# A mask product over 160 instead of 224 columns, with the scores laid out by head and a new fixed order of operations

## Chip, core and metric

The kernel runs on one core of one Trainium2 chip. The metric is the device time of one execution in microseconds (us); lower is better. The core has five engines that work side by side, each through its own queue, in order: TensorE (PE, matrix products), ScalarE (ACT, functions and copies), VectorE (DVE, elementwise work and 32x32 block transposes), GpSimd (POOL) and SyncE (SP), which mostly issues DMA transfers. They hand work to one another through semaphores.

## What is computed

Two attention branches over the same 2048 tokens of width 512, mixed by a gate `g`. The part that matters here is branch A: 64 segments of 32 tokens, one after another. Each segment puts 8 memory rows ahead of its tokens, attends over these 40 rows in 32 heads of 128, and hands its first 8 output rows on as the memory of the next.

```python
idx = jnp.arange(L)                                   # L = 8 + 32
mask = (idx[:, None] < M) | (idx[:, None] >= idx[None, :])
for s in range(n_seg):
    h = jnp.concatenate([mem, x[:, s * seg_len:(s + 1) * seg_len, :]], axis=1)
    q, k, v = (jnp.einsum('btd,dhe->bhte', h, W) for W in (Wq, Wk, Wv))
    scores = jnp.einsum('bhqe,bhke->bhqk', q, k) * scale
    scores = jnp.where(mask[None, None], scores, -1000000000.0)
    p = _softmax(scores, axis=-1)
    o = jnp.einsum('bhte,hed->btd', jnp.einsum('bhqk,bhke->bhqe', p, v), Wo)
    mem = o[:, :M, :]
    outs.append(o[:, M:, :])
...
return g * a + (1 - g) * b
```

Branch B is a causal attention in four stretches of 512 tokens with a linear memory, 32 heads of 16. It has no chain from segment to segment of 32 tokens, so its pieces can be put between those of branch A.

## The kernel before

Every piece of work is an operation with a name, an engine (or a choice of engines), a function that issues its instructions, what it reads and writes, and a cost and due time for a planner (`Prog`). The order of operations on each engine does not come from the planner's due times here: it is given outright, as a packed list in `ORDER`, which `sequences` unpacks; an operation that may run on two engines runs on the one in whose list it stands. `schedule` then walks through the lists in the planner's model of time (`LATENCY`, `TO_PE`, the costs), by which it hands out the eight PSUM banks and picks between two forms of some products. `emit` writes the instructions and the waits. So the model's constants count twice: when an order was searched for, and when banks are handed out.

**A segment** (`p_seg`), for each half `r` of 16 heads: `k`, `q` and `v` are projected (`wproj`, L1399), 4 column groups of the array side by side, copied out (`kev`, `qev`, `vev`, L999) and k and q transposed on DVE (`ktp`, `qtp`, L1464). In `p_s` one PSUM bank takes the scores:

- `H` (L1472, a helper at L1022 or L1024) multiplies a constant `neg` (-1e9 on a diagonal) with a constant `hide` (ones where a score is masked), and so writes the mask into the bank.
- `S` adds the scores: 16 products of 40 queries with the segment's own 24 tokens and 8 memory rows (L1479), and 4 products of the last 8 tokens' keys, whose projections are made four segments at a time (`rk`, `rq`, `rv`), with the last 16 queries (L1483).
- `exp` (ScalarE, L1487) turns the 224 columns into `PT`: columns 0 to 159 are the 4 heads' 40 queries against the own keys, 160 to 223 the 4 heads' 16 late queries against the remaining keys.

In `p_u`, `U` sums over the keys by a product with ones (L1502); `ln` and `rc` (ScalarE, L1506 and L1508) form the reciprocal as exp(-ln); `nrm` (DVE, L1510) and `nrr` (DVE or POOL, L1513) scale `PT`. `PV` (L1544, L1549) multiplies with the values, `OTev` copies out, `wo` (8 operations, L1298) projects back, `par` and `fold` add the partial sums, and `hm` (L1321) writes the memory rows of the next segment, on which its `k`, `q` and `v` depend.

**Branch B** runs in 16 units: projections `bk`, `bq`, `bV`, logits `bL` (L1139), exponentials `bE` (L1157), triangle masks `bM` on POOL (L1163), `bPV` (L1180), and outputs. Its `bL` pieces share PSUM banks with `PV` in many segments.

**The start.** The weights arrive in the first 50 us or so. PE meanwhile runs 64 products without use (`warm`), early work of branch B and the first projections. `tables` (L782) sets up ScalarE's function table for exp, ln and copies.

Of the kernel before, what the change touches and what calls it, by code (L numbers as in the profile page):

```python
# [8 lines left out]
ALU = mybir.AluOpType  # L9
# [6 lines left out]
    "c-nPZ2S5|&+kf6%lFK3qLs4;|f`D6aQ>!9cC$?gtPPAA@t<+t`g(4MKwQg-4t+wdjja6JI?g1+9i56E~pb!#5a_@cbU6RXP@Ix}Vd+wRPXT9wRxdE(TE7QZ&WVFaSec^ly"  # L16
    "W0(U;D`4TH*ZW(weG>Aa#pLw&KXpC!y~?{dy}d0aZNZOAUtd1a<wTo)(=rQ_mdnh_@jv;t3*XRd$FJ7cS#WkO1e@{#3#w@2nT2&9FI`mtN?1Ki0~6=Z8Ld7VeKZ=D#BSHb"
    "T#3jC+5oE?M4xN_<)rCpuT>VHSzSg?3k@0HK;%g(0svHLbIw9|c4t_1z>KgQmPVYOb}Tot?Xb2@sY?^jM6R{T!)}9bl{>Zng}P7bC}nzp^Fh9W=f1pUq^>vjE2qIya=k3Z"
    "VggW`9~w?B+Yh04PK;Uy5uJ!U;C~K5Yo9}{FAY`L5Jh>}?O?eK5ys+cZDnvKQhlULy#p;=q%go|-Jc_Ut&D=HVzsCuk9tu>DljkGjO#v!!de9u2w4{^Fg^f%vhY|dQrHaS"
    "8Zv*ZE-zNy*H;J4?K;Y<Z|b%(gUUg97|LS~1H>w93fteK+MhF%YX(c(3y6HGLvQ3<o+mI(0{CUJEt8=cq5=@Y*R?GMo1J<Djc*2?gU?Sv%@E>o$4|Ar(8eD?juZ?-bkJ2O"  # L20
    "Z04dsdx=W^^nbAp@71pjuLRQq0G7pmb6Q7PX>IYxDsO7ZA44sQDkrYf!Lk_(U`ocnse&5$08MHgjAkf`Suz*QUO-vOG-ZTR{WM?zK$c)yry0=o7;L)C5Uyz9OqCoys?El7"
    "vu=J`+5CC`+nQs6=o|;>jSis~^G9xoVGi^|UKUk}+`9-gcFInHQkG5b|FuovN|c4d9yh(M423?dSpbFL1Kxpf1;TFv3cW+TX3s!_1wZUbj9>LVz)^%~E7B?|6d%=3gYWyj"
    "tz}-@zmW+R!Hfkba|G(I^IGnx-;z*M$Yub!o%-POUaqK6eXRD%D}5#{c<lNFIALl{RH$LnzVNNM6{!EHrpwE`O1#vm0fV*yj27Hg2jIzzxIzu0d|y{BFV!<<_|G3yO1oLD"
    "-UuxrH#}?&z<7amdT?;)U(JRRoKaeUGVm_anrM&#Y#M9-ZKA+7WsYIpL|#pc%Az)F<#Uo$KLeze0w`(09tD6^so^j{(=x`QD+L0WUnVV?Rkj3va+_22P<ZYa-bAFKRCgq>"
    "iRD3cE@_?x!@ZXF>%nl&=QBZW`pR)D3k}nM<9NQS2djFITj}fbUfnbwm4a4l3cDTlFb!a~z<MIA8?~f+qb$xIZ!0Kl@?s-;-{pjQPxsDnYs;YR3!e(SFOpX){kHEA`O$I!"
    "Hx|=C5<yd@bnEIvUT<U0>KWQ*_^417RC@&>6{WzrDDsTD<)zls63C;fpa&fB+^_+2_HjsEGm~TtL8-A=C7TC3ADKWI4DeDAy)g{hjc5ZY2vLj|m?v&1@h0glE7f&6scwC)"
    "{Z<%qMbKaz#J7)`GJ>$xTC6Pq9t1rsBLz$OmZZzr)g)T4_4`H=9Y+4alg9)6^WjkWcs>n$E6hC(sp*?Fp!=!MVM8++iI+cQLn}}NDRuzIAO}+RT-(R_t4EGSh00*XctZu)"
    "snp~h!)BzUK&lYkQ6#)8yb^ZuN-HYNdRrOE8=XzQaBkw-mmA%L*C~6moAy2=V-$3$j^rU2?G=`YoAQPPoXfvor3Uy;FfRz;esIEOt;uM~=&Rj6$m_X}YBgNlSf-QP>?F_s"
    "`nF8D|J4-Yy7a0113T|Gj%n6^8wr|Msg6W#=g49LHrXaf(5y;O-Xs*w1?E?t#-4=)im}lhZre?CIVhXmkd+#OZ)-Aohdz2uC~62=KLn_+yB5uPf+E!%R2IXJ=?uw)w%6?~"
    "x!Yx+PFn7&361}$Mc$RwCrwh==vMh)DUZCox1V8i>Wzid7EVu_PC%4#d$|zsOIwDu9@AwChYb?%-(ZBAE>fE{9M~GeJ$D8X*3U9WTND-rNuhFDUaI11?r4BN2d@PYEH6M?"  # L30
    "Q**{ZmD-S=tBIHEk%DDL8Y1>R?EO)Y>pgYpn<@k-jKZs!(#bz+NXT>#0?n@)Xg<p>e*ojo2`qmCNc-!?KdA0=#;cfC$xDa_v{XjSuCFy)2Tn~{1~5xdbJ9E5y#44=J_bwX"
    "m`U~$q$ALp#5x}Ckq^BIRyadS6e_yHqy?M&@R#<U<mM59S8e#UZ*9<US;+ZaSE{0I_QydbuYw*l%?~?7DEbJre*?s2C}&s@rLd@!x#8tE8yoTf8p7RB(Aq6<4*GFnIz>n$"
    "Ir=~-Ftt=5E2?t3^(AO?vAQ?u{v>y7q?xNpsZ`!<Oqezo_@DY<fR6eD@uYYo1-V+TT0dG|thH0CVT{`T%T92orBCn7_oO)JXe-g>?@{II)uRfks~?3HubEpyZr^LN=OH9J"
    "8BbdXQ#X9GdThrWhs!8V3!1Lr(DkUX{f-@=1xI?e14lg>dUiT_5H^!`jtE#<!6i~0NcuF+hT3JiQW8)9z=AReE8uz89FjJ@?=VOGHj`3s<g($P-kdk8f~$>@#Jd~vf?_Dz"
    "riBkmzTLsg0F}%{$^mg0Pjm(%k8aOlx@GeT5P2bG-g`Bq&ME<a6Db(i_RcL3U^RFYKzrlCc#`6zbjm-1nx2qeqBiRw@Kv>Eq%puuQGy2@3<B(!40u@4#G_|BlFqr)-8hlq"
    "&qN0|z7P}jWbmkoz5EeC8$oPsfTv&Py>Jz54t1Yh=3qycH-9O#Y`$dsJ?YHBEYne7ffK4>wkCjP<>>NFVYjCWJO=`7+qd(WOSaBV7lDezMP27nebVh+R(S0=$<?1D3Jb-J"
    "3?zPr3VVyI9HD)4lE96Og&(NB!_o4|q@jQC1(3ZnT7gV9{&I`T#S5A0IK{oLs*_tNJ3r3YY07z@=8Y)i3Jg?v^QO@)XmqQkm-VBb8&q_qIx<L~gC2*Xj{CHeJ0CegUR0e!"
    "5b_e6u)H%y-;l%!yF%&)<RoBp_qnC{EExV8qjfk4ieUGT7<K9a6=!lWin@YPWb<obx#17MM*Gs(0Qj@_*zY=YEXl{wV7US9?}V-%55&(kb|jK1Q>O;YsXkz*Wq5=SY+XM="
    "!5GP<1@JT2$_)szY5Xk#uTfo2E5U9dSF{IkBAGaiYbJt44>oA@5NS=bGGlg=;nG27QmV+MM*L%7k*mR$(;dJ!c2{7tJdQ}Fgd+bkjXiyqS1CN<$3Z<IH2Z^11xQ;m_A=Av"
    "nr+d78OzFPo-la{!qK;?Fz>1&eMwa)Qr&AsG$yL_#xJZ)VGH&B;38F{Lh?8QjUTScflBA#Xrfc+k&Bmlasv;iPKEEQYO`mm5!N*!Ls-BIy_yrkJ-RW;)Sjf3j;N=E>x~Ek"  # L40
    "wSFsMDf7n&q~j_w0R$&hlkyAjbCJ;{p-QRW+qyh^&iZ-NX_>a9HOXRQNsnBf#BRCQ8W64p{{0RRvch1_b0#uZ;jiIYw?nj3SNk7}?h~@R(b&sr0Fj7QGCUM+5RmDghHzwd"
    "N)Am5OtbX+PDN5287Gv)s?NV!)0Bf;Lw7pU-u^0Rzl6KQzYbnD;M5;D6ptbk5YfI!)hUmWnG6JP$6*#XHJnx#8~K2d&5PQm`{>K_;x4Gs)Rm=;9juB}M6Z>TWLTHJ-^xr|"
    "jP%bAOys?2x8(F8A~sZo8>FclNvt@r<(noDcTZ_k>uECAzSm9SJ#3;?2y69lHHt{)6(p9)@HhA|GQVzMGk&NBo8q~r7o-Eyls4s2!r5ByK9^LQ+H3Jpg$Qw=O*+i{k-$C2"
    "L#f;#)08gQ$%Ub+GYUqcMh4^`t_#l`;nQ;$39m^Jcp7r~k_3h@%L*tQgD8E8R^xC02M1Fd5wdKz!ilMkQ(+P^I<z+tR@!DZ^e}=q&{l5D4Ttm<p!qAo>Y(8fI_`9bD^`k6"
    "1101&Ar)IQbtA6Y^|+Ha?{3|+<e&$^l#W<aq|#v-m<&i)dS~Ar9#`)|!4jEIBpOJf)#0MT(-BY^WH`T^1h_jsPU+Onpcn|M>R>M>W1!#*&cr_Wk)mAYRE%VV)(0yoC-4aG"
    "ZWl><`Z<*%DZpocy}&-1PKa@_*_=dtkcq!zT+i{0bY43k#X|9%Ie-xw1sKtCNaCa8aD&#5a{CgLns#rh62vg%zMRY!1ol%$Y>GP-BY#t+y2^S#L~~je+3)F%v`nNeyGRzv"
    "Cv{=?rsn5g_P%9Nz4aTq6`HmiyBhUMo}Ds#@%DjvP;(C?Uc0jSLMiMSZ2NoYXA8HlXn#EF+}7W&;~M`_{<dQ8T7`p1VeP)Y?o(*sJ7z(<^G#KDHQ95HfBvok?3;QYD7bhf"
    ";?4v(JfNBdtX>TE!8WB_ex-AE7pQ5ae@{?hjJ;JA)U^nI69VJTks8uGm|LOVGP&FUUN#+>mKgl|B%2N=t*ZYf3ntzSQ(bL_(<ghAp~5Do@;YVw2)cU>ZCZ>A1H2c`ppJDv"
    "Qmq40T6e(UBjYg<@E^?5ZImf+R<DD(OD<@8KdDXH>|9tnaj}i2e)#cy_l~oonqXC_8c38CnDW})AKH9OnMtVhHl+fe?3((zWca3C{r}k-8~e<HE0AVp%IvYLm!IzcoTiRJ"
    "_al8Wzk*$4kvI)+Yha`=taYzRMcO<)e0>IJj9Wd#<ua{}Hr9DcL;c5fl?ZoP-TG1snwpnV5&$#yuK2KkE>|GC7p203Hr;OdOP$O?{b0}C#i6)Dhtb#--o$B#p;z#-crx>)"  # L50
    "CLcRN*e;%EggI#yDpFI8Wj-Vi4)ny{Hf_c7pA5O-O)(LY8--7xF7nVn-^R^I`wQZORD`OacK_ns_th)Zv%B^fv_1ZB^^UJYY_bX+FuH;UA@>#dG<<i@3uX4Mu3Da?K$!8K"
    "o}!g|U2hIy7)RVd_(d2dZp#7`2S2u1Ho^DZV&W&ecV-NgxH)0>sEXaiK|r31XuFm39YuUPX!Q28SXrjUp*Ow11=tEDm!pp|RK2DUKR`bUFPc@V!Ny6;<UR<FOs4VY7l4^{"
    "HV<SJWcCFe$}Y^^`7)58hl5I^yVQs+Q`g17g?2aZH)wl?q{<)TY@v@hw5Z!!#;r(N17iRZ0)kI=InizY-2IBLAp?ru>>^o3)O^_pQxuh#Q@RA2C~>*U?)|=oRbH##s$&iB"
    "4KYFfLO4fb8Y8>+^)Q;6w0t<g4z2MyG;2B_x%hPxW;S$d$3#4$sAJik+tu7P<#8zI=;WG-oae`!7`g)1PbbFnsD|O&Y;|AFyq`rTm?}hhH3RorUmCVWA4<ueZ&?U>KO*W;"
    "AUAQy<k!O6u8bNKJNtSY=rp?<Fy!&`ovd=|_*aW3?;fY(&JyNL_pbk}V!~Pj#GRCpsYl1DNl_;O*<$wrGze+QQCY5b|8WtSoibytyd0Df*U2|mWv2)TN#<QukPdLDY8Qk5"
    "y{2TWy3-Kj{LevYtG~5#&HWwyU&9_4xnY9JV$%@qNsN<LE%+JLq6%7?L5Y7G?rqcMw#e!U2T9~J0-mQPrz$v)hBYW49_<X-`fe)t=!>wSKG<K7a0GfeJV{aVBe5ZOt7GM&"
    "so0S8D^PMTl(0F}CTnx8c^+E6C4N32`SJ0vy(5B*8%<|mI|<e7Uu=_C$YJWofZ53_!QiI?y40!H=}vnMs1F=Sq%jY@&h68v8!fKBi5<R4&U?zvRS&O%dR1f)bSm{Ik79~C"
    "(M=Dv$rJNu+Bq&%<GwjJ;xe>BG;JmV8S>2O&e^^2p+0)}aDae_Sv!FNEd}qY+f)XS8H@cnanB(1PH4rWrj#K&+6)^1ns8MXPK<u<r?egEi_fAclpPrmqiC7;c*sE@c{TPI"
    "J7rH<aIwR?(^+4{oU%p@3rgPYd!*xeXf-AOER4&$9MlExw+*PX6QgR3chQq(0RLN8gZ`i~+&cXGi;6j4wes$Ix<hXjGi7Ie@9z&i2<mk=q(C|D%Y6_rs6%@g*s(2~KXn)P"
    "?sR@h@^_bV)2`+8Non3I>+;2w_t%Y$>o`1gSwi^tw~~epyPg}bDOo=C_)PqMBS2>u@-!IF+SEw7W^9$J_37QqF2@f?JJ;0i6<NQ`JFD;cA^2A^;V=I3N{1RFPSG1`_G^08"  # L60
    "r^hjX>DO>9{j5Ptm>>OhtK2K+x2)@2^I7-IpRa5hGrH94*Z3n(w$JIF1zTHxJC5$DZ(H6t`o+}#7rM6?`a^JidiBFKBQ}hT%gFyX@2^LD)~-$3`)>K~>(G`SwCYdWhSLdj"
    "7W9S|sqnDDw$}Mf-0<~nVHrgC>3mK#46e5LY{>ETC~fc67K@-qpCw;4tbZ(ZYfi_(QO93bt$lrII<(sp5P1f=G-}i-ejNIJLva7c53(*cU)?TmPBp*y?_ltsFAfwZp6V99"
    "2w+X___3qo+Tpk=!%)r78(9jo(+|g}!f@o8anEx4G{Xx4);CF<OxLa-_uu&+)}fhAGD07pT#z#@Z{m=njnj*JE*igV!Mo=tzJOYdj0t%-9896fvGkd!It5+nDo3Ly&1~6z"
    "d53VnxA_g>-nUKQ9=+rrTGj5%(%RWp81jdO4*t!m?fX7ydCzIP`Y%O`Q$gPR`lRecb<#qaOty?)W6U5dT;ylW+&OdS0IY@~qt<U3wq>x4t>BIWHUU`2l27j3KA|`4?bD4r"
# [504 lines left out]
FLEX = ("c32", "full")  # L569
# [13 lines left out]
class Kernel:  # L583
# [194 lines left out]
    def p_init(self):  # L778
        P, C, M = self.P, self.C, self.M
        op, dma = P.op, P.dma  # L780
# [640 lines left out]
    def p_seg(self, s):  # L1421
# [13 lines left out]
        def bank():  # L1435
            return P.slot("A")
# [31 lines left out]
        def p_s(r, i, prio):  # L1468
            rb = bank()

            def f_hide(pe, m):
                return self.mm(pe, m, pb[rb.b][:, 0:224], self.neg[:, :], self.hide[:, :], True, True, skip_group_check=True)  # L1472
# [137 lines left out]
```

## Time and profile before

| | |
|---|---|
| runs | 833.68, 831.29, 832.03 us; median 832.03 |
| span of the profiled execution | 828.3 us |
| DMA, first 52 us | busy share 0.99, 373 GB/s |
| mask product, tiled form (L1022, 128x224) | x504 matmuls, mean 259 ns a row |
| function table loads on ScalarE | 2, of 1.28 us, at 1.31 and 12.86 us |
| nrr on POOL, on DVE (L1513) | x90 at 371 ns; x38 at 238 ns |

The span runs from the first to the last recorded instruction; the time of a run has something more around it. A row of the profile gives an instruction's line, engine, operation, tiles (out<-in) and its partitions by elements. A matmul's row lasts until its results are out, but the next may start much earlier, so for PE the step from start to start is what counts.

### The profile page before, as it was taken

To read this page: it belongs to the slowest core of one execution; us is meant where nothing else is said; L and a number is where in the kernel's file an instruction comes from. 1 tells how busy PE (TensorE), PEld (TensorE's weight loads), DVE (VectorE), ACT (ScalarE), POOL (GpSimd) and SP (SyncE) were. 2 spreads that over 40 slices of the span, in tenths; PEclk is the share of its full clock that TensorE was granted. 3 is DMA by queue.
4 is the path that set the end of the run, shared out by engine and by line. 5 is a ranking of instruction groups with operands and counts; after the bars stand their busy time and mean duration, and the time that the engine had idled before them with its cause. 6 is when DMAs were issued, how large, how long until landed. Compare 5 with 4: busy or idle time off the path is not lost.

```text
span 828.3 us, 53292 instructions
## 1 busy us (share of the span) xinstructions
PE 804.8 (97%) x24456; PEld 521.1 (63%) x24474; DVE 617.3 (75%) x1398; ACT 564.1 (68%) x1279; POOL 262.3 (32%) x576
## 2 busy tenths in 40 slices
PE   8999999999999999999999999999999999999987
PEld 4445666766666566666767666666666665666654
DVE  4788668769778767778687687776877767876775
ACT  4677766777767666676667766677666677767663
POOL 3552231223323323223233233423223223323340
PEclk9999999999999999999999999999999999999999
DMA  9982111111111111111012111100111110010001
GB/s 344 413 248 58 41 26 39 38 45 31 42 30 30 33 28 43 28 34 46 26 33 53 38 27 31 34 22 11 49 38 39 34 26 8 13 26 21 21 21 36
DMA packets 71701, 45.63 MB, mean 55 GB/s; under 512 B 50046, under 2 KB 69942, under 8 KB 69942
## 3 DMA queue, kind: packets, MB, share of 16 engines
q1 hardware_dynamic: 70422, 41.18, 17.2%
q8 instruction: 192, 3.15, 1.6%
q10 hardware_dynamic: 1056, 1.05, 0.4%
q14 instruction: 31, 0.25, 0.1%
HBM read 30.72 MB, written 8.87 MB: 48 GB/s over the span
## 4 chain that ended last, share of the span: by engine, by line
PE 86%; DVE 4%; ACT 4%; DMA 3%; issue 1%; SPq 1%; POOL 1%; DVEq 0%; POOLq 0%; ACTq 0%
PE pb L1399 47%; PE pb L1298 17%; PE pb L1022 7%; PE pb L1139 3%; PE pb L1544 3%; PE pb L1180 2%; PE pb L1024 2%; DMA st<-in_A_mem_dram 2%; PE pb L1502 2%; PE pb L1479 1%; DMA out_dram<-stg 1%; PE pb L1228 1%; ACT rc_sb L1508 1%; ACT rc_sb L1506 1%; PE pb L1483 1%
## 5 line engine op out<-in xcount | busy, mean ns | idle before, releaser
L999 ACT ACTIVATE st<-pb 128x512 bf16<-128x512 f32 (+2 forms) x313 | 149.1, 494 | 103.5 <-PE pb L1399 78.3
L1157 ACT ACTIVATE PTB<-pb 128x640 bf16<-128x640 f32 x240 | 158.4, 703 | 35.2 <-PE pb L1139 30.3
L1399 PE MATMUL pb<-Wv_sb,hT 128*32 128x512 bf16 x2048 | 162.7, 380 | 0.1
L1399 PE MATMUL pb<-Wq_sb,hT 128*32 128x256 bf16 (+1 forms) x3072 | 139.4, 308 | 0.1
L1399 PE MATMUL pb<-Wk_sb,hT 128*32 128x512 bf16 x2048 | 133.2, 379 | 0.2
L1298 PE MATMUL pb<-Wo_sb,OT_sb 128*32 128x256 bf16 x4096 | 131.9, 273 | 1.0 <-DVE OT_sb L999 0.4
L1513 POOL TENSOR_TENSOR PT_sb<-PT_sb,rc_sb 128x64 bf16<-128x64 bf16 x90 | 33.4, 371 | 248.2 <-ACT rc_sb L1508 239.7
L1163 POOL TENSOR_SCALAR_AFFINE_SELECT PTB<-PTB 128x512 bf16<-128x512 bf16 x120 | 77.8, 649 | 105.7 <-ACT PTB L1157 99.2
L1298 PEld LDWEIGHTS pb<-Wo_sb,OT_sb 128*32 128x32 bf16 x4096 | 100.7, 96 | 15.6 <-ACT OT_sb L999 3.8
L1399 PEld LDWEIGHTS pb<-Wq_sb,hT 128*32 128x32 bf16 x3072 | 83.3, 97 | 39.8 <-issue 1.9
L1464 DVE STREAM_TRANSPOSE QT_sb<-st 128x256 bf16<-128x256 bf16 (+1 forms) x192 | 94.4, 510 | 17.1 <-ACT st L999 15.2
L1464 DVE STREAM_TRANSPOSE KT_sb<-st 128x512 bf16<-128x512 bf16 x128 | 89.4, 700 | 12.2 <-ACT st L999 10.5
L1399 PEld LDWEIGHTS pb<-Wk_sb,hT 128*32 128x32 bf16 x2048 | 57.7, 97 | 43.0 <-issue 1.7
L999 ACT ACTIVATE OT_sb<-pb 128x320 bf16<-128x320 f32 (+1 forms) x140 | 58.2, 428 | 37.7 <-PE pb L1549 36.4
L999 DVE CAST OT_sb<-pb 128x320 bf16<-128x320 f32 (+1 forms) x120 | 56.9, 479 | 31.4 <-PE pb L1549 29.6
L1399 PEld LDWEIGHTS pb<-Wv_sb,hT 128*32 128x32 bf16 x2048 | 52.8, 97 | 17.8 <-DVE ao L1328 0.6
L1506 ACT ACTIVATE rc_sb<-pb 128x160 f32<-128x160 f32 x128 | 38.9, 304 | 35.5 <-PE pb L1502 34.5
L1321 DVE CAST hT<-pb 128x32 bf16<-128x32 f32 x63 | 12.0, 191 | 66.7 <-PE pb L1022 66.5
L1487 ACT ACTIVATE PT_sb<-pb 128x224 bf16<-128x224 f32 x128 | 45.7, 357 | 17.3 <-PE pb L1483 12.6
L999 DVE CAST V_sb<-pb 128x512 bf16<-128x512 f32 x65 | 44.5, 685 | 9.9 <-PE pb L1399 8.9
L1510 DVE TENSOR_TENSOR PT_sb<-PT_sb,rc_sb 128x160 bf16<-128x160 bf16 x128 | 42.7, 333 | 8.1 <-ACT rc_sb L1508 6.8
L999 ACT ACTIVATE stg<-pb 128x512 bf16<-128x512 f32 (+1 forms) x68 | 37.9, 559 | 13.6 <-PE pb L1399 9.6
(204 smaller groups left out, 1468.9 us busy)
## 6 DMA issues: line engine op xcount, KB each, us to landing
Wv_sb<-in_A_Wv_dram SPq DMA_DIRECT2D x4, 1024.0 KB, 11.3
Wk_sb<-in_A_Wk_dram SPq DMA_DIRECT2D x4, 1024.0 KB, 20.2
Wq_sb<-in_A_Wq_dram SPq DMA_DIRECT2D x4, 1024.0 KB, 26.1
Wo_sb<-in_A_Wo_dram SPq DMA_DIRECT2D x4, 1024.0 KB, 21.3
rest_v<-stg SPq DMA_DIRECT2D x112, 32.0 KB
rem_v<-rest_v SPq DMA_DIRECT2D x28, 128.0 KB, 3.1
a_rows<-ao SPq DMA_DIRECT2D x63, 32.0 KB
stg<-a_rows SPq DMA_DIRECT2D x15, 128.0 KB
```

The source lines that it names most:

```text
L999: self.P.op(("act", "dve"), (lambda a: a.activation(dst, src(), ACT.Copy), lambda d: d.tensor_copy(dst, src())), reads=reads, writes=write ...
L1022: ins = pe.matmul(out[32 * c:32 * c + 32], lhsT[:, 32 * c:32 * c + 32], rhs, start=start, stop=stop, tile_position=(0, 32 * c), **kw)
L1139: ins = pe.matmul(pb[slot.banks[i]][:, base + a - lo:base + b - lo], KT[r0:r1, 128 * kc:128 * kc + 128], Q[r0:r1, t0 + a:t0 + b], start=Tr ...
L1157: P.op("act", (lambda dst=dst, src=src: lambda a: a.activation(dst, src(), ACT.Exp, scale=0.25))(), reads=[pair], writes=["%s%d_%d" % (nam ...
L1163: P.op("gp", (lambda pt=pt, ii=ii: (lambda g: g.affine_select(pt, pt, ([[0, len(ii)]] if len(ii) > 1 else []) + [[1, 128]], ALU.is_ge, 0.0 ...
L1298: ins = pe.matmul(pb[so.b][p0:p0 + 32, 0:256], tok(r, g, l), self.Wo[:, h, 256 * d:256 * d + 256], start=(r == 0 and g == 0 and l < 2), st ...
L1399: ins = pe.matmul(self.pb[sl.b][32 * g:32 * g + 32, 0:hi - lo], x[:, c, 0:32], cols, start=(c == 0), stop=(c == C - 1), tile_position=(0, ...
L1464: op("dve", (lambda dst=dst, src=src: lambda d: d.transpose(dst, src))(), reads=["st%d%s" % (i, tag)], writes=["%sT%d%s" % (kind, r, tag)] ...
L1487: op("act", lambda a: a.activation(PT[:, r, :], pb[rb.b][:, 0:224], ACT.Exp, scale=SCALE), reads=[rb], writes=["PT%d" % r, "PT%dr" % r], n ...
L1506: op("act", lambda a: a.activation(rc[:, r, :], pb[rb.b][:, 0:160], ACT.Ln), reads=[rb], writes=[rr], name="ln%d_%d" % (s, r), cost=t_act( ...
L1510: op("dve", lambda d: d.tensor_tensor(PT[:, r, 0:160], PT[:, r, 0:160], rc[:, r, :], ALU.mult), reads=[rp, rr], writes=[rp], name="nrm%d_% ...
L1513: op(("dve", "gp"), tuple((lambda e: e.tensor_tensor(rest, rest, late(rc[:, r, :]), ALU.mult)) for _ in range(2)), reads=[rp + "r", rr], w ...
```

## The change

1. **Layout.** `PT` and the scores' bank hold, for each of the 4 heads, 56 columns: first the 16 late queries against the remaining keys (`rest`), then the 40 queries against the own keys (`mine`). Every product that reads or writes them goes through these views.
2. **Mask product.** The queries that mask nothing (the memory's and the last 8 tokens' against the own keys) now lie at the end of each head's columns. `H` writes columns 0 to 39 of each 56, 160 columns in all, and `hide` shrinks to 160.
3. **The planner's model.** The hand-over times grow by 0.02 us on PE, ScalarE, DVE and POOL (`LATENCY`), and by 0.015 from ScalarE to PE; the cost of `H` falls to 0.072 and that of `nrr` on POOL rises to 0.42.
4. **The order.** `ORDER` is another list. Compared by operations: PE has the same 2914 in another sequence, tiled forms for 127 of the 128 `H` (126 before). ScalarE has 1258 operations (1283 before), DVE 1466 (1398), POOL 529 (572), SP 367 as before, in much the same sequence. `nrr` runs 58 times on POOL and 70 on DVE (90 and 38 before). `tables` stands after 66 operations in ScalarE's list (after 3 before). The built program has six function table loads on ScalarE where it had two: the first at the start, then ahead of `ln0_0`, of `bE1_6_3`, of `ln0_1`, of `rc0_1`, and `tables` itself between `OTev0_0` and `OTev0_2`.

```diff
-    LATENCY = {"pe": 0.22, "act": 0.04, "dve": 0.04, "gp": 0.1, "sp": 2.0}
-    TO_PE = {"pe": 0.0, "act": 0.015, "dve": 0.06, "gp": 0.05, "sp": 0.0}
+    LATENCY = {"pe": 0.24, "act": 0.06, "dve": 0.06, "gp": 0.12, "sp": 2.0}
+    TO_PE = {"pe": 0.0, "act": 0.03, "dve": 0.06, "gp": 0.05, "sp": 0.0}
...
-        self.hide = t("hide_sb", [128, 224])
+        self.hide = t("hide_sb", [128, 160])
...
-        hide = [("hide", self.hide[0:32, lo:hi].rearrange("p (h q) -> p h q", h=4)) for lo, hi in ((0, 160), (160, 224))]
+        hide = self.hide[0:32, :].rearrange("p (h q) -> p h q", h=4)
+        hide = [("hide", hide[:, :, lo:hi]) for lo, hi in ((16, 40), (0, 16))]
...
+        def by_head(t):
+            return t.rearrange("p (l q) -> p l q", l=4)
+
+        mine, rest = [by_head(PT[:, r, :])[:, :, 16:56] for r in range(2)], [by_head(PT[:, r, :])[:, :, 0:16] for r in range(2)]
...
-                return self.mm(pe, m, pb[rb.b][:, 0:224], self.neg[:, :], self.hide[:, :], True, True, skip_group_check=True)
+                return self.mm(pe, m, by_head(pb[rb.b][:, 0:224])[:, :, 0:40], self.neg[:, :], self.hide[:, :].rearrange("p (h q) -> p h q", h=4), True, True, skip_group_check=True)
...
-                        ins = pe.matmul(pb[rb.b][32 * g:32 * g + 32, l * L:(l + 1) * L], KT[:, 16 * r + 4 * g + l, :], QT[:, 16 * r + 4 * g + l, :],
+                        ins = pe.matmul(pb[rb.b][32 * g:32 * g + 32, 56 * l + 16:56 * l + 56], KT[:, 16 * r + 4 * g + l, :], QT[:, 16 * r + 4 * g + l, :],
...
-                    ins = pe.matmul(pb[rb.b][32 * g:32 * g + 32, 160:224], Kr[:, h0:h0 + 4].rearrange("p h k -> p (h k)"), QT[:, h0:h0 + 4, 24:40],
+                    ins = pe.matmul(by_head(pb[rb.b][32 * g:32 * g + 32, 0:224])[:, :, 0:16], Kr[:, h0:h0 + 4].rearrange("p h k -> p (h k)"), QT[:, h0:h0 + 4, 24:40],
...
-                    for k, (dst, src) in enumerate(((o[:, 0:160], PT[:, r, 0:160]), (late(o[:, 0:160]), PT[:, r, 160:224]))):
+                    for k, (dst, src) in enumerate(((by_head(o[:, 0:160]), mine[r]), (late(o[:, 0:160]), rest[r]))):
...
-            op("dve", lambda d: d.tensor_tensor(PT[:, r, 0:160], PT[:, r, 0:160], rc[:, r, :], ALU.mult), reads=[rp, rr],
+            op("dve", lambda d: d.tensor_tensor(mine[r], mine[r], by_head(rc[:, r, :]), ALU.mult), reads=[rp, rr],
...
-               writes=[rp + "r"], name="nrr%d_%d" % (s, r), cost=(0.235, 0.33), prio=prio)
+               writes=[rp + "r"], name="nrr%d_%d" % (s, r), cost=(0.235, 0.42), prio=prio)
```

`PV` reads `mine[r]` and `rest[r]` in the same way. The 67 lines of `ORDER` become 63 others.

## Prediction

> **What bounds the kernel now.** I read the page first, then the timelines of TensorE (PE) and ScalarE (ACT) over single stages, then the waits.
>
> ```profile
> span 828.3 us, 53292 instructions
> PE 804.8 (97%) x24456; PEld 521.1 (63%) x24474; DVE 617.3 (75%) x1398; ACT 564.1 (68%) x1279; POOL 262.3 (32%) x576
> PEclk9999999999999999999999999999999999999999
> PE 86%; DVE 4%; ACT 4%; DMA 3%; issue 1%; SPq 1%; POOL 1%; DVEq 0%; POOLq 0%; ACTq 0%
> ```
>
> PE is busy 97% of the span at full clock and is 86% of the chain that ended last; no other engine passes 75%. Busy hides small stalls, since a matmul's row lasts longer than the step to the next one. So I read the steps, in PE's timeline of a middle segment:
>
> ```profile
> 309.30 0.27 PE L1022 MATMUL pb<-hide_sb,neg_sb 128*32 128x224 bf16 x4
> 309.39 0.27 PE L1479 MATMUL pb<-QT_sb,KT_sb 128*32 128x40 bf16 x16
> ...
> 310.40 0.39 PE L1399 MATMUL pb<-Wv_sb,hT 128*32 128x512 bf16 x4
> 310.62 0.27 PE L1502 MATMUL pb<-PT_sb,ones_sb 128*32 128x160 bf16 x8
> 310.71 0.39 PE L1399 MATMUL pb<-Wv_sb,hT 128*32 128x512 bf16 x4
> ```
>
> A row lasts 0.27 or 0.39, but the next starts 0.09 or 0.22 later: four column groups run side by side, and columns set the step. Laid beside the operations in their planned order, the trace gives each step: 95 ns for a mask product of 224 columns, 215 for four matmuls of 512, 97 for a sum U (160 and 64 columns). Take each step at the low tenth of its kind (operation, arrangement of the array, arrangement of the next): together 779.7 us. What is over that is 43.5 us of stalls: 5.7 before 48 us, 1.0 from 48 to 65, 34.0 from 65 to 800, 2.9 after. So a column taken away counts almost in full, and so does any new stall.
>
> **The change, part by part.** I take the sum against the span, 828.3; the median shown, 832.03, lies 3.7 above it, for what lies around the span.
>
> *Mask product.* From 224 to 160 columns. The steps 95 (224 columns) and 215 (512) differ by 120 ns over 288 columns, 0.417 ns each; 64 columns are 26.7 ns, and 128 products give 3.4 us. Lower end nothing (a step that only uncovers a wait), upper end 3.4. I take -3.4, since nearly all 126 tiled products are at 95 or 96 ns, with no wait in them.
>
> *Layout.* PT is now read and written in runs of 40 and 16 with a stride of 56. On PE the late score block already reads its queries in runs of 16 (L1483, 196 ns a row) and the sums' second product reads runs of 64 (L1502, 193): no price. On VectorE (DVE) the product L1510 takes 333 ns for 160 elements and L1513 238 for 64, whose rc operand already comes in runs of 16: 1 ns an element both ways, no price. On GpSimd (POOL) L1513 takes 371; the nearest copies are 280 (96 elements) and 435 (256, strided), so -0.09 to +0.06 each. It is off the path but where PV waits for it: some 26 stalls, 3.3 us together, so -2 to +2; I take 0.
>
> *The order.* All 2914 PE operations remain, in another order. Priced with the same steps, the new list is 779.4 without the mask cut, against 779.7 (arrangement switches, about 107 ns each, go from 388 to 385): -0.3. Stalls are the open item. For each hand-over I added up the PE work between producer and consumer, in both orders, and what it lacks of the time the hand-over took in the trace (low tenth of all):
> scores to U: 2.1 us lacking in all before, 1.5 after; U to PV: 11.0, 10.1; v to PV: 6.5, 4.7; last wo to fold: 2.8, 1.6; PV to wo: 4.0, 3.6; fold to the next k or q: 0.8, 1.0; q and k to scores: 3.2, 3.3.
> Together 30.4 against 25.8, 15% less. Of the stalls, some 22 us end with a hand-over from ACT, DVE or POOL; 15% of these is -3.4. Bounds: +3 (25 copies leave ACT and 32 of the L1513 products leave POOL for DVE, which gets 68 operations, some 25 us, and would be 78% busy: transposes wait in its queue), and -8 (a third of 22).
>
> *The table loads.* This the diff does not say. The operation that sets up ScalarE's function table stood fourth in its queue and now stands after 66 others, behind the first softmax. In the built program ScalarE has six table loads where it had two: one at the start, as before, and five in segment 0: ahead of ln0_0, ahead of the exponential that follows (bE1_6_3), ahead of ln0_1, ahead of rc0_1, and the set-up itself between OTev0_0 and OTev0_2. The planner has no cost for the first four. In the trace of before, in ScalarE's timeline:
>
> ```profile
> 11.54 1.30 ACT L1157 ACTIVATE PTB<-pb 128x640 bf16<-128x640 f32 x2 [8.95 <-PE pb L1139]
> 12.86 1.28 ACT L782 ACT_TABLE_LOAD   x1
> 14.19 1.30 ACT L1157 ACTIVATE PTB<-pb 128x640 bf16<-128x640 f32 x2
> ```
>
> The load starts where the exponential ended (12.84) and takes 1.28; there it cost nothing, as the next input came at 14.13. In segment 0 ScalarE and PE run so:
>
> ```profile
> 48.96 0.40 ACT L1487 ACTIVATE PT_sb<-pb 128x224 bf16<-128x224 f32 x1
> 51.22 0.30 ACT L1506 ACTIVATE rc_sb<-pb 128x160 f32<-128x160 f32 x1 [0.33 <-PE pb L1502]
> ...
> 53.81 0.30 ACT L1506 ACTIVATE rc_sb<-pb 128x160 f32<-128x160 f32 x1
> 54.15 0.34 ACT L1508 ACTIVATE rc_sb<-rc_sb 128x160 f32<-128x160 f32 x1
> 54.49 0.44 ACT L999 ACTIVATE OT_sb<-pb 128x320 bf16<-128x320 f32 x1
> ```
> ```profile
> 48.11 0.28 PE L1479 MATMUL pb<-QT_sb,KT_sb 128*32 128x40 bf16 x16
> ...
> 58.34 0.39 PE L1298 MATMUL pb<-Wo_sb,OT_sb 128*32 128x256 bf16 x8
> ```
>
> From S0_0 (48.11) to the last wo of the segment (58.34) PE takes 10.2 us, 9.4 of it work; ScalarE has almost no gap. With the new order, from S0_0 at X: exp0_0 ends at X+0.8; two exponentials to X+2.0; load to 3.2; ln0_0 to 3.55; load to 4.8; bE1_6_3 to 5.3. Its triangle mask on POOL (0.65) and a hand-over (0.145) let bPV1_1 start at X+6.15, where PE has come to X+2.8: 3.3 us idle. U0_1 follows at X+7.0; on ScalarE rc0_0, bkexp2, two exponentials and exp0_1 last to X+7.5, load to 8.7, ln0_1 to 9.05, load to 10.3, rc0_1 to 10.7, OTev0_0 to 11.0 (wo0_0 waits, PE idle 2.3 more), load to 12.3, OTev0_2 to 12.75; wo0_4 goes at X+12.8, the last wo at X+13.8. PE's work in this stretch is 7.9 in the new order. Stall 5.9 against 0.8: +5.1. PE works in order and its work after is the same, so nothing gives it back. Queued behind each load is all of ScalarE: exponentials, evictions, and through them DVE and SP's stores. Lower end 2.6 (only the two loads between an ln and its exponential bite), upper end 6.4 (five whole loads).
>
> Sum: 828.3 - 3.4 - 0.3 - 3.4 + 5.1 = 826.3 in the span; with 3.7 around it **830.0 us**.
>
> The Trainium skill, "ScalarE: Activation LUTs", section "What ACT_TABLE_LOAD costs", gives about 1.28 us for the load, which the trace confirms, and adds a drain of 1.38, 2.66 a switch. In the row above the load begins 0.02 us after the exponential ended and the next instruction 0.05 after the load, so no such drain shows; by the page's figure five would be 13.3, and the sum about 837.
>
> **Rivals.**
> *A, the forecast:* loads bite by some 5 us, stalls shrink by some 3; 827.5 to 832.
> *B, the order gains more.* The covers shrink evenly and the big stalls go too: 23 of over 0.3 us between 65 and 800 us make 11.8 us. Gain 8 rather than 3.4: 825.4. For it: short covers fall in most kinds. Against: many of the 23 end with no engine's hand-over, and so are not the order's to remove.
> *C, the loads hide.* ScalarE reaches a load while it would wait for PE anyway. Two or three hidden: 2.6 instead of 5.1, 827.5; for it, loads need no input; against, ScalarE's queue in segment 0 is full.
> *D, slower: the table switches starve PE.* If a switch also empties the pipeline, up to one 0.70 exponential each, five give 3.5 more; and if the idle of 3.3 us lowers PE's clock, 3.4 us at half clock cost 1.7, twice 3.4: 830.0 + 6.9 = 836.9. It decides once idle in segment 0 passes some 8 us. Against: in 22 to 26 us PE was busy 2.9 of 4 us and the granted clock stayed 1.00. The Trainium skill, "TensorE: Matmul & The Clock Gate", Part 1, lets the clock fall to half after an idle window of about 3.4 us; only the tail of this trace shows it (0.84 after the last matmul).
> *E, slower: DVE's load.* Its added 25 us make the transposes late in each segment: 3 us more stalls rather than 3.4 less, 836.4.
>
> **How the numbers follow.** Chances: A 0.47, B 0.20, C 0.13, D 0.12, E 0.08. Within 0.3% (2.5 us, 829.5 to 834.5) is about what a measurement of this kernel can tell from no change. A gives same 0.30, faster 0.12, slower 0.05; B and C faster 0.30, same 0.03; D and E slower 0.17, same 0.03: faster 0.42, same 0.36, slower 0.22. Range 825.0 to 836.5, which leaves out the ends of B and D; A alone is 827.5 to 832.
>
> **What would show it.** The mask product's step falls from 95 to about 69 ns, all else of PE's steps as before. ScalarE's timeline shows six table loads, five of them in some 10 us in segment 0, and PE's busy share falls there, with idle before L1180 and L1298 that before has not. From 65 to 800 us PE's stalls are about 30 us instead of 34. I am wrong if the loads lie in time ScalarE waits anyway, if the granted clock dips below 1.00, or if L1464 starts later after its copy than now.

## The result, and the profile after

The kernel became slower. The median of four runs is 839.59 us (838.47 to 840.74); the kernel before, run beside it, took 831.92 (831.29 to 833.68). The ratio is 1.008, 95% interval 1.0054 to 1.0106: some 7 us more, where 2 us less was forecast. The profiled execution is the run of 838.47; its span is 836.7, so about 1.8 us lie outside the span. (The forecast put 3.7 there. Before's span of 828.3 thus belongs to an execution of about 830.1, 2 us quicker than its median. Single executions of one kernel spread by some 5 us, so below medians decide the size and a profile only the place.)

The page of after, the same lines as shown of before:

```profile
span 836.7 us, 53305 instructions
PE 806.3 (96%) x24492; PEld 526.1 (63%) x24492; DVE 636.5 (76%) x1466; ACT 559.0 (67%) x1258; POOL 242.6 (29%) x533
PEclk9999999999999999999999999999999999999999
PE 84%; DVE 4%; ACT 4%; issue 3%; DMA 3%; SPq 1%; POOL 1%; DVEq 0%; POOLq 0%; ACTq 0%
```

Nothing new bounds the kernel: PE still leads, VectorE is at 76%, the clock's digit is 9 in every slice. One share has grown: "issue", time in which PE waited for nothing that the profile shows, is 3% of the chain instead of 1%.

PE's rows (start, duration, engine, line, operation) in a middle segment of after show the edit itself doing what it should:

```profile
319.83 0.26 PE L1019 MATMUL pb<-hide_sb,neg_sb 128*32 128x160 bf16 x4
319.90 0.62 PE L1396 MATMUL pb<-Wq_sb,hT 128*32 128x256 bf16 x16
...
321.65 0.26 PE L1019 MATMUL pb<-hide_sb,neg_sb 128*32 128x160 bf16 x4
321.72 0.44 PE L1019 MATMUL pb<-V,phiK 128*32 128x136 bf16 x16
```

The next operation starts 0.07 us after the mask product, 0.09 before. By all rows the step is 69 ns against 95. With each step at the low tenth of its kind, as in the forecast, PE's work fell from 779.7 to 776.0 us. The stalls grew from 43.6 to 55.0: +5.4 up to the last `wo` of segment 0, +6 after it.

ScalarE in segment 0 of after:

```profile
50.68 1.28 ACT L1508 ACT_TABLE_LOAD   x1
51.97 0.30 ACT L1508 ACTIVATE rc_sb<-pb 128x160 f32<-128x160 f32 x1
52.29 1.28 ACT L1154 ACT_TABLE_LOAD   x1
53.59 0.44 ACT L1154 ACTIVATE OT_sb<-pb 128x320 bf16<-128x320 f32 x1
...
56.22 1.28 ACT L1508 ACT_TABLE_LOAD   x1
57.52 0.30 ACT L1508 ACTIVATE rc_sb<-pb 128x160 f32<-128x160 f32 x1
57.84 1.28 ACT L1510 ACT_TABLE_LOAD   x1
59.13 0.34 ACT L1510 ACTIVATE rc_sb<-rc_sb 128x160 f32<-128x160 f32 x1
59.38 0.42 ACT L996 ACTIVATE OT_sb<-pb 128x320 bf16<-128x320 f32 x1
59.81 1.28 ACT L778 ACT_TABLE_LOAD   x1
61.11 0.44 ACT L996 ACTIVATE OT_sb<-pb 128x320 bf16<-128x320 f32 x1
```

Five loads of 1.28 us, where the forecast put them. What follows each starts 0.01 to 0.02 us after its end. From `S0_0` to the last `wo` PE took 13.8 us, as the forecast had it (X+13.8), against 10.2 before.

The waits of PE after the first 65 us are the surprise. Two stretches of the weight-load rows of after and before (the last bracket is the idle time and what ended it):

```profile
301.23 0.13 PEld L1019 LDWEIGHTS pb<-xT,wkB_sb 128*32 128x32 bf16 x5
302.83 0.10 PEld L1019 LDWEIGHTS pb<-xT,wkB_sb 128*32 128x32 bf16 x3 [1.47 <-issue]
302.84 0.32 PEld L1295 LDWEIGHTS pb<-Wo_sb,OTr_sb 128*32 128x32 bf16 x8
```
```profile
316.36 0.65 PEld L1399 LDWEIGHTS pb<-Wk_sb,xr 128*32 128x32 bf16 x16
317.98 0.39 PEld L1022 LDWEIGHTS pb<-fold_sb,st 128*32 128x32 f32 x16 [0.97 <-DVE QTm L1062]
```

In the first, PE stops in the middle of one operation, after five of its eight products, whose data are all there: 1.47 us for nothing that an engine owes it. In the second an engine is named that had long been done. Both lie at the same place in another count. Count PE's instructions in order: a product is two (load of weights, matmul), one of the f32 fold four, a wait on a semaphore that is an instruction of its own one (335 on PE in the built program of after; the other waits ride on a product). Then the long stops of this kind stand at numbers that leave 193 or 194 when divided by 256, in both kernels, over the whole span. The page has the matching queue:

```profile
q8 instruction: 192, 3.15, 1.6%
```

192 packets, 3.15 MB, or 16 KB each: one for each block of 256 instructions. Laid beside the block ends of after, the packet that starts after one block end is what PE needs at the next: it had landed at least 1.2 us before PE went on, at every block end, and no packet is fetched two blocks ahead. For the stop above: block end at 298.32, packet from 300.09 to 301.45, PE on at 302.83. So a block has a floor: from its start to the packet's start (0.4 to 2.0 us in nine cases of ten), the transfer (0.9 to 1.4), and 1.2 more, about 3.4 us on average and up to 5. PE's own time for a block, without that wait, is 4.0 at the middle and 3.3 for the shortest twentieth. Where the block is quicker than its packet, PE waits.

The Trainium skill, "Runtime: NRT & Kernel Launch", section "Instruction fetch mechanics", describes blocks of 256 instructions fetched by a queue of the engine's own, and calls the cost of crossing into the next "mostly hidden". The block size agrees with the count; the cost does not: up to 1.5 us at one crossing here.

Added up after 65 us, the waits at block ends (the gap in a profile wherever the packet had landed less than 1.7 us before) are 7.1 us in before and 16.2 in after. That is a reading; the experiments test it.

### The profile page after: what moved, and what is told of

Read it like the earlier page. It is cut to its first block, busy times and chain, and to the rows that moved or that the text cites. A ratio compares the mean times of both kernels' runs of the same rounds, so it can differ in the third digit from the quotient of the medians.

```text
span 836.7 us, 53305 instructions
## 1 busy us (share of the span) xinstructions
PE 806.3 (96%) x24492; PEld 526.1 (63%) x24492; DVE 636.5 (76%) x1466; ACT 559.0 (67%) x1258; POOL 242.6 (29%) x533
## 3 DMA queue, kind: packets, MB, share of 16 engines
q8 instruction: 192, 3.15, 1.6%
## 4 chain that ended last, share of the span: by engine, by line
PE 84%; DVE 4%; ACT 4%; issue 3%; DMA 3%; SPq 1%; POOL 1%; DVEq 0%; POOLq 0%; ACTq 0%
PE pb L1396 46%; PE pb L1295 17%; PE pb L1019 7%; PE pb L1136 3%; PE pb L1545 2%; PE pb L1177 2%; DMA st<-in_A_mem_dram 2%; PE pb L1021 2%; PE pb L1504 1%; PE pb L1481 1%; PE pb L1485 1%; DVE V_sb L996 1%; PE pb L1225 1%; ACT rc_sb L1508 1%; PE pb L1550 0%
## 5 line engine op out<-in xcount | busy, mean ns | idle before, releaser
L996 ACT ACTIVATE st<-pb 128x512 bf16<-128x512 f32 (+2 forms) x302 | 143.8, 496 | 106.0 <-PE pb L1396 89.6
L1396 PE MATMUL pb<-Wv_sb,hT 128*32 128x512 bf16 x2048 | 159.0, 380 | 0.0
L1396 PE MATMUL pb<-Wq_sb,hT 128*32 128x512 bf16 (+1 forms) x3072 | 142.0, 308 | 0.5 <-DVE hT L1318 0.3
L1466 DVE STREAM_TRANSPOSE QT_sb<-st 128x256 bf16<-128x256 bf16 (+1 forms) x192 | 94.7, 510 | 12.1 <-ACT st L996 10.3
L996 DVE CAST OT_sb<-pb 128x320 bf16<-128x320 f32 (+1 forms) x116 | 54.8, 478 | 20.6 <-PE pb L1550 19.5
L1514 POOL TENSOR_TENSOR PT_sb<-PT_sb,rc_sb 128x64 bf16<-128x64 bf16 x58 | 20.6, 355 | 165.0 <-ACT rc_sb L1510 164.0
L1568 POOL COPY OTr_sb<-OT_sb 128x256 bf16<-128x256 bf16 x55 | 23.0, 419 | 94.6 <-DVE OT_sb L996 61.2
```

Source lines behind the costliest of these rows:

```text
L996: self.P.op(("act", "dve"), (lambda a: a.activation(dst, src(), ACT.Copy), lambda d: d.tensor_copy(dst, src())), reads=reads, writes=write ...
L1396: ins = pe.matmul(self.pb[sl.b][32 * g:32 * g + 32, 0:hi - lo], x[:, c, 0:32], cols, start=(c == 0), stop=(c == C - 1), tile_position=(0, ...
L1466: op("dve", (lambda dst=dst, src=src: lambda d: d.transpose(dst, src))(), reads=["st%d%s" % (i, tag)], writes=["%sT%d%s" % (kind, r, tag)] ...
L1568: op("gp", lambda g: g.tensor_copy(own[:, :, 8 * (s % 4):8 * (s % 4) + 8], OT[:, :, :, SEG:L].rearrange("p g h k -> p (g h) k")), reads=[" ...
```

## The experiments

Each was timed beside the kernel before; ratios are to it, with 95% intervals.

| kernel | median us | ratio | waits at block ends after 65 us, in its one profile |
|---|---|---|---|
| before (in the three sets) | 832.2, 832.9, 832.9 | 1 | 7.1 |
| after | 839.6 | 1.008 (1.0054 to 1.0106) | 16.2 |
| `a_tables` | 833.9 | 1.0009 (0.9992 to 1.0025) | 12.9 |
| `b_tables` | 837.7 | 1.0068 (1.0049 to 1.0088) | 10.4 |
| `b_layout` | 832.2 | 0.9998 (0.9984 to 1.0012) | 11.2 |
| `a_oldlayout_t` | 834.1 | 1.0015 (0.9999 to 1.003) | 9.9 |
| `b_layout2` | 830.3 | 0.9966 (0.9947 to 0.9986) | 8.9 |
| `b_cols40` | 826.1 | 0.9928 (0.9898 to 0.9957) | 10.3 |
| `a_t_plus64` | 845.2 | 1.0142 (1.0109 to 1.0174) | 25.8 |
| `a_t_minus12` | 828.7 | 0.9952 (0.9938 to 0.9966) | 10.1 |
| `a_t_minus24` | 827.7 | 0.9925 (0.9896 to 0.9954) | 9.4 |
| `a_t_minus36` | 826.6 | 0.9935 (0.9913 to 0.9957) | 9.5 |
| `b_l2_plus64` | 845.8 | 1.016 (1.0135 to 1.0184) | 23.9 |
| `b_l2_minus24` | 830.5 | 0.9975 (0.9959 to 0.9992) | 9.5 |

**The table loads.** One operation moved in ScalarE's list, out of after and into before:

```diff
+        q = out["act"]
+        q.insert(3, q.pop([o.name for o in q].index("tables")))
         self.ops = out
```

In `b_tables` the place is 66.

> The kernel after, with one operation (tables) put back to fourth place in ScalarE's list; everything else as in after. Theory T (the late set-up brings four more table loads, and the stall of segment 0 with them, and nothing later gives it back): two loads in ScalarE's timeline, PE's stalls up to the last wo of segment 0 fall from 11.9 us to about 6.8, median 839.6 - 5.1 = 834.5 us, still above before by about 2.5. Rival (PE would be as late without the loads, since later waits swallow the gain): 839 or so, with the 5 us turning up again as stalls after segment 0.

> The kernel before, with the same operation moved to place 66, as in after. Theory T: six loads, five of them in segment 0, median 832.0 + 5 = 837 us. Rival (the loads bite only in the new order of ScalarE's queue): 832 to 834.

Both as theory T had it: 839.6 falls to 833.9 without the late set-up, and before rises by 0.68% (5.7 us) with it. PE's stalls up to 65 us fall to 6.5 from 11.9 in the profile. The windows of after and of `a_tables` (bounds, length, then busy us of PE, PEld, DVE, ACT and POOL; clock, DMA share, GB/s) show what else came with the loads:

```profile
52.00:56.00 4.00, 2.31 (x53) 1.28 (x57) 1.39 (x4) 3.97 (x8) 0.58 (x2) 0.88 0.83 234
56.00:60.00 4.00, 3.40 (x68) 1.19 (x60) 1.21 (x4) 3.92 (x7) 0.64 (x1) 0.69 0.24 54
```
```profile
52.00:56.00 4.00, 4.00 (x131) 2.37 (x132) 3.27 (x9) 2.43 (x7) 1.09 (x3) 1.00 0.87 255
56.00:60.00 4.00, 4.00 (x128) 2.56 (x124) 2.04 (x7) 2.42 (x5) 1.51 (x3) 1.00 0.38 77
```

ScalarE is full while PE is busy for little more than half of the first window, and the granted clock falls to 0.88 and 0.69, which is 3.4 us at 0.5. In `a_tables` it stays 1.00 there. The same holds beyond these two profiles: the mean clock of an execution is 0.996 to 0.998 in the four of after and 0.994 to 0.996 in the six of `b_tables`, and 1.00 in all twelve of `a_tables`. In the profile of `b_tables` the half clock lasts 6.8 us, from 57.6 us on. From `S0_0` to the last `wo` PE takes 13.8 us in after and 8.7 in `a_tables`, 5.1 more with the loads; in the old order it takes 16.9 in `b_tables` and 10.2 in before, 6.7 more.

**The layout and the mask product alone**, in the order of before; then the order alone, in the old layout.

`b_layout` is after with `ORDER`, `LATENCY` and `TO_PE` of before. `a_oldlayout_t` is before with those three of after, and `tables` at place 3. `b_layout2` is `b_layout` with two more costs of before (the planner's cost of `H`, and that of `nrr` on POOL):

```diff
-            op("pe", f_hide, reads=["neg", "hide", "st%d" % i], writes=[rb], name="H%d_%d" % (s, r), cost=0.072, prio=prio, mode=FLEX)
+            op("pe", f_hide, reads=["neg", "hide", "st%d" % i], writes=[rb], name="H%d_%d" % (s, r), cost=0.1, prio=prio, mode=FLEX)
...
-               writes=[rp + "r"], name="nrr%d_%d" % (s, r), cost=(0.235, 0.42), prio=prio)
+               writes=[rp + "r"], name="nrr%d_%d" % (s, r), cost=(0.235, 0.33), prio=prio)
```

> The new layout and the mask product of 160 columns in the order of operations of before, with the planner's constants of before; two table loads. Theory: the product's step falls to 69 ns and 128 of them give 3.4 us, stalls as before: 832.0 - 3.4 = 828.6 us. Rival 1 (what a column saves comes back as a wait for the next hand-over or the next block of instructions): 831 to 832. Rival 2 (strided reads of PT cost VectorE or GpSimd something): above 832.

> The new order and the new constants of the planner, with the old layout and mask product of 224 columns, and the table set-up early: the order alone. Theory F (PE takes its instructions in blocks of 256, and in the new order the ends of the blocks fall where PE runs through a block too fast, some 6 us more than before between 65 us and the end): 839.6 - 5.1 + 3.4 = 838 us, with gaps of PE of 0.4 to 1.6 us at every 256th instruction. Rival H (the forecast's own term: hand-overs shrink by 3.4): 832.0 - 3.7 = 828. Rival L (the stalls come from the new layout): 832.

> Again the new layout and the mask product of 160 columns in the order of before, now with every cost in the planner as in before, so that banks and waits are those of before and only the columns and the layout differ. Theory F (a block of 256 instructions takes PE at least 3.2 to 4.8 us, by when its fetch starts and lands; time saved inside a block that is already at that floor is lost, time saved in the others is kept): of 182 blocks some 15% are at the floor, so some 0.5 of the 3.4 us is lost, and another 0.6 as a longer wait ahead of S: 832.2 - 2.3 = 829.9 us. Rival P (the plan's changed banks cost b_layout its gain): 828.8. Rival Z (a column of the mask product is worth nothing at all, because PE waits for what follows): 832.2 again.

`b_layout` gained nothing, a miss. Its planner, given a shorter `H`, had handed out other banks and put in one wait instruction more on PE (342 instead of 341). With the plan of before, `b_layout2` gains 0.34%, 2.8 us of the 3.4 (1.2 to 4.4 by the interval): rival Z is out, theory F and rival P both fit. Why the other banks and the wait cost some 2 us was not traced further. The order alone, at 834.1, is near neither 838 nor 828. Theory F's figure counted on the layout's full 3.4 us, of which 0.2 shows in this order (834.1 and 833.9); that the order alone is no gain, as rival H had it, is plain. Rival L's 832 lies within this run's interval; but in the new order the old layout is no faster than the new (834.1 and 833.9), and in the old order the new layout gains or is level, so the layout does not bring the stalls.

**The value of a column.** The same instructions in the same order, with 40 of the 224 columns. The mask of the other columns is left out, and the products of `S` that now come first there start their columns (`start=True`, in the part not shown):

```diff
-                return self.mm(pe, m, pb[rb.b][:, 0:224], self.neg[:, :], self.hide[:, :], True, True, skip_group_check=True)
+                return self.mm(pe, m, pb[rb.b][:, 0:40], self.neg[:, :], self.hide[:, 0:40], True, True, skip_group_check=True)
...
```

> The kernel before, with the old layout, whose mask product writes 40 of the 224 columns (the mask of three heads in four and of the late keys is left out; the first product into each other column starts it afresh). Same instructions in number and order. The product's step should fall from 95 ns to about 30: 128 x 65 = 8.3 us less work. Theory F: about 75% of it arrives, 832.2 - 6.2 = 826 us. Rival Z: 832. If b_layout2 shows no gain and this one does, the loss lies in the new layout and not in the columns.

The step fell to 28 ns, 8.5 us less work; 0.72% or 6.0 us of it arrived (3.6 to 8.5 by the interval). So about seven tenths of the time saved at this product reaches the end, in agreement with theory F's 75%, though the interval is wide; a column is not worth nothing.

**Where the blocks end.** A few products without use near the start are cut into more pieces or issue fewer, so that every later block end moves along the list of operations.

```diff
...
-                return pe.matmul(pb[sw.b][:, 0:512], self.phiK[:, 0, :], self.phiQ, start=True, stop=True)
+                n = 1 if isinstance(pe, Count) else {16: 16, 0: 16, 9: 3}.get(i, 1)
+                for j in range(n):
+                    lo, hi = 32 * j, 32 * j + 32 if j < n - 1 else 512
+                    ins = pe.matmul(pb[sw.b][:, lo:hi], self.phiK[:, 0, :], self.phiQ[:, lo:hi], start=True, stop=True)
+                return ins
```
```diff
...
+                    if m == "c32" and not isinstance(pe, Count) and (k, c, i) in [('v', 0, 3), ('v', 2, 2), ('v', 2, 6), ('v', 2, 8)]:
+                        return pe.matmul(pb[sw.b][0:32, 0:512], part[:, 0:32], part, start=True, stop=True, tile_position=(0, 0))
                     return self.mm(pe, m, pb[sw.b][:, 0:512], part[:, 0:128], part, True, True)
```

The first is `a_t_plus64`: `a_tables` with three warm-ups in 16, 16 and 3 pieces; `b_l2_plus64` does it to the first three of its order. The second is `a_t_minus24`: four fillers, six instructions fewer each; `a_t_minus12` takes two, `a_t_minus36` six, `b_l2_minus24` four of its own order. The `b_l2` kernels start from `b_layout2`. The planner (`Count`) sees no difference, so banks and waits stay.

> The kernel after with the tables set up early, and with 64 more instructions of PE in the first 5 us (three idle warm-up products cut into pieces, the same columns in all), so that every later block of 256 ends 64 instructions earlier in the order of operations. Theory F: worked out from the trace of the kernel without the shift (its steps without the waits at the ends of blocks, and the spread of the time that a fetch took in six traces), the waits at the ends of blocks should go from 9.7 to 15.1 us: 833.9 + 5.4 = 839.3. Rival H (waits come from hand-overs; where a block ends is of no account): 834 to 835.

> The same with 24 fewer instructions of PE in the first 30 us (four idle warm-up products use one column group in four). Theory F, worked out in the same way: 8.0 instead of 9.7 us at the ends of blocks, the lowest of all shifts: 833.9 - 1.7 = 832.2 us. Rival H: 834.

> As the kernel with 24 fewer instructions, but with 12 fewer (two warm-up products cut to one column group). Theory F (the planner counts PE's instructions to place the ends of blocks, and its count falls behind the real one: by 12 at 190 us, 25 at 340 us, 28 later; a shift that undoes this puts the ends where the order wants them): between no shift and the shift of 24, 829 to 832 us. Rival O (the gain came from the cut products themselves, about 1.5 us each): 833.9 - 3 = 831; this kernel alone does not tell them apart, the next does.

> 36 fewer (six warm-up products cut). Theory F: past the best place, 828 to 830 us, no faster than 24 fewer (827.7). Rival O: six products cut, 833.9 - 9 = 825.

> The order of before with the new layout (its costs as in before), with 24 fewer instructions of PE in the first 25 us (four warm-up products cut). Theory F: in this order the planner's count is right to within 12 up to 450 us and only then falls 23 to 33 behind, so the shift helps the second half and harms the first: a gain of 0 to 2, 828.3 to 830.3 us; the new order, put right, stays ahead or level (827.7). Rival O: -6, 824.3.

> The order of before with the new layout, with 64 more instructions of PE at the start. Theory F: both orders were made for the ends of blocks where they are; waits at the ends of blocks go from 8 to 15 us by the trace's steps, and by what the new order showed (11 us for the same shift) perhaps more: 830.3 + 7 to 11 = 837 to 841. Rival N (only the new order is sensitive): 830 to 832.

This settles that the place of the block ends counts. 64 more instructions at the start, which cost no columns, make the new order 11 us slower and the old one 16; 24 fewer make the new one 6 us faster and leave the old one as it was. Six fillers cut gain no more than four (ratios 0.9935 and 0.9925), and four in the old order gain nothing, so the gain is not the cut work's own (rival O); nor does the chain of segments start earlier with them: `S0_0` begins at 48.6 and 48.7 us in the profiles of `a_tables` and `a_t_minus24`. The waits view of PE (engine, tile, line, what ended the wait: us in total, times, longest) of `a_tables`, `a_t_minus24` and `a_t_plus64`, the lines with "issue" of 0.5 us or more:

```profile
PE pb L1021 <- issue: 3.9, 6, 1.1
PE pb L1023 <- issue: 1.4, 9, 0.2
PE pb L1297 <- issue: 1.0, 2, 0.8
```
```profile
PE pb L1400 <- issue: 1.2, 3, 0.6
PE pb L1299 <- issue: 0.6, 2, 0.3
PE pb L1023 <- issue: 0.6, 2, 0.4
PE pb L1229 <- issue: 0.5, 1, 0.5
```
```profile
PE pb L1025 <- issue: 10.5, 19, 1.0
PE pb L1402 <- issue: 1.8, 3, 1.0
PE pb L1487 <- issue: 1.5, 1, 1.5
PE pb L1301 <- issue: 1.5, 5, 0.4
```

L1021, L1023 and L1025 are, in this order of the kernels, the same line of one helper, through which the f32 fold and products of branch B go (L1023 of `a_tables` is the helper's other form). The fold issues 32 instructions in some 0.15 us, so a block that holds one and little slow work is short.

The directions came as theory F had them; the sizes missed, most of them too small: by the trace +64 should have cost 5.4 and -24 gained 1.7, `a_t_minus12` and `a_t_minus36` came out 0.3 and 1.4 us below their ranges and `b_l2_plus64` 5 us above its own. The estimate from the trace drew each fetch time from one pool for all blocks. In the profile of `a_t_plus64` a fetch after a block end with a wait of over 0.3 us took 3.75 us to PE's going on, the others 3.43: waits breed waits, and the estimate has none of this. Nor does it have what a shift does elsewhere: from `a_tables` to `a_t_minus24` the waits at block ends fell by 3.5 us, and the stalls at hand-overs, in the same order, by another 2.5 (22.2 to 19.7). Whether these two are all of the gap stays open.

Why -24? The planner holds a count of PE's instructions and places block ends with it (`BLOCK_AT`, `EXTRA`). Laid against the real count, its own falls behind in both orders: in after by 12 at 150 to 225 us, 25 at 300 to 375, 28 from there on; in before by 5, 11 and 12, and by 23 to 33 only after 450. So in after nearly all block ends lie some 25 instructions from where the order was made for them. A shift of -24 undoes that. In the old order the shift should mend the second half and put the first, which was in place, out of it. In the profiles of `b_layout2` and `b_l2_minus24` the stalls from 65 to 200 us are 3.0 and 4.8, from 500 to 800 us 20.6 and 18.3. The other unshifted profiles of this order have about 3 in the first stretch and some 17 to 22 in the second, so the harm is clear of their spread and the mending is not.

## Why the prediction was wrong

*Mask product.* Right in the step (69 ns) and, with the plan held, close in the time: 2.8 us of 3.4. In the new order without a shift only 0.2 shows, with some 2 us of uncertainty.

*Layout.* Right. `nrm` 334 ns (333), `nrr` on GpSimd 355 (371).

*Table loads.* Right in the mechanism and near in the size: 5.1 forecast, 5.7 by the medians, five loads in 10 us of segment 0. The drain that the Trainium skill adds to a switch ("ScalarE: Activation LUTs", "What ACT_TABLE_LOAD costs") is absent from the rows and from the time. Rival D's clock did fall, in every execution with the late set-up, and that was one of the forecast's signs of being wrong. In the profile of after the 3.4 us at half clock lie where ScalarE is full, and the stretch of segment 0 grew by the 5.1 us that the forecast had without them; in that of `b_tables`, with 6.8 us at half clock, it grew by 6.7. So part of the 5.7 may be the clock's; how much was not separated.

*The order.* Here it failed: "15% of these is -3.4". Same layout, tables early, the new order (with the constants and banks of its planner) against the old, `a_tables` against `b_layout2`, is 1.0009 / 0.9966 = 1.0043 (1.0017 to 1.0069 from both intervals): +3.6 us, where -3.4 and another -0.3 for the switches were forecast. The step that failed is that the order was let change only the stalls that end with a hand-over, and all other stalls were taken as fixed. In the profiles of these two kernels the waits at block ends grew from 8.9 to 12.9 us, and that is more than the hand-overs gave back. From 65 to 800 us, where the forecast looked for about 30 us of stalls instead of 34, after and `a_tables` have some 40. The forecast saw such stalls: it said of the 23 big ones that many "end with no engine's hand-over, and so are not the order's to remove". They are the order's, since it decides which operations share a block; and they were its to add. The planner's constants for blocks were in the code, and the forecast did not lay them beside the trace.

The hand-over term itself had the right sign, but came to 1 to 2 us instead of 3.4. The stalls within 0.3 us of an engine's hand-over, after 65 us and without block ends, are 23.2 and 24.2 us in the profiles of the old order (before, `b_layout2`) and 22.3 and 22.2 in the new (after, `a_tables`): ahead of the fold 2.9 became 1.0, ahead of PV about 8.5 became 6 to 7, while ahead of the next q and k and of S about 2 us were added, where the forecast had 0.3. With 24 instructions fewer they are 19.7, and the new order against the old is then 0.9925 / 0.9966 = 0.9959 (0.9924 to 0.9994), a gain of 3.4 us. That this equals the forecast's figure is partly luck: it sets the best of the shifts tried in the new order beside the old order in its own place.

*The sum.* 832 - 2.8 (layout) + 3.6 (order) + 5.7 (loads) = 838.5, and 839.6 was measured. How layout and order share the +0.8 depends on which comes first: in the old layout the order costs 1.2 (`a_oldlayout_t`, -0.1 to 2.5), and the layout then gains 0.5 by the ratios. Rivals B, C and E are out: the loads don't hide, the order never gained 8 (a figure that the forecast called a third of 22, which is 7.3), and waits for hand-overs did not grow by 3 as in E; the transposes start on average 285 ns after the end of their copy after 65 us, 301 before. D's 836.9 is the rival nearest to the measured time, but not by D's way: it had no stalls from the order, and the emptied pipeline that makes half of its extra does not show.

`a_t_minus24`, the change with the set-up early and 24 instructions fewer, beats both kernels: 827.7 us, 0.9925 of before.

## What to carry to other kernels

A stall with no engine behind it, above all one in the middle of an operation, is to be counted in instructions: if such stalls stand at one remainder of 256, PE is waiting for its instructions, and runs of short operations have to be spread over blocks. Where an order has been tuned, any edit that adds or drops a few instructions early shifts all that follows, and can cost more than it saves (here up to 16 us for 64 instructions); try a few shifts before judging an edit of a few tenths of a per cent. And look in the built program for table loads, which the diff here did not show.

## What the hardware showed that was not expected

That the supply of instructions sets a floor of some 3.4 us on average for 256 of them on PE, and that the fetch of a block waits for the block end before it (0.4 to 2.0 us after it in nine cases of ten). Fetch times differ from run to run, which may be why executions of one kernel spread by 5 us; that was not tried. The clock has a smaller part in it: in the three sets of before, the executions with a mean clock of 0.999 or less have medians 0.9 to 1.6 us above the others, while the others alone still spread by 2 to 5 us. As for the clock itself, two idle stops of PE (1.42 and 1.36 us, between 50.9 and 54.1 us in after) were followed by 3.4 us at half clock, from about 55 us by the windows above, though no single stop lasted longer than 1.42 us.
